# Gate and val of a fused attention and MLP kernel, by 15 products for three token blocks and three weight groups instead of 7 products for two and two

## The chip, the core and the metric

The kernel runs on one core of a Trainium2 chip. The metric is device microseconds of one execution. The engines are named as in the profile: PE multiplies matrices into PSUM (8 banks of 128 x 512 float32), DVE, ACT and POOL do elementwise work, SP issues every DMA of this kernel from one queue, in program order; a DMA is carried out by 16 DMA engines. Each engine runs its own instructions in the order in which they stand, and waits on semaphores for the others.

## What is computed

Blockwise attention (chunks of 64 keys) feeds two MLP layers. The change is in the second, the gated one: gate and val are two products with the same input, of width 1536.

```python
def _moe_ref(x, w_in, w_out):
    h = np.maximum(x @ w_in, 0.0)
    return (h * h @ w_out).astype(np.float32)

def _moe2_ref(x, w_gate, w_val, w_out):
    gate = 1.0 / (1.0 + np.exp(-(x @ w_gate)))
    val = x @ w_val
    return (gate * val @ w_out).astype(np.float32)

# x: 4608 tokens x 512; w_in 512 x 2048, w_out 2048 x 512
# w_gate, w_val 512 x 1536, w_out 1536 x 512
```

All inputs and results are float32, the weights in the layout of 64-bit words from which the kernel makes float32 itself.

## The kernel before

Every float32 product is made of three products of split operands: `split` (L466 to L487) has ACT round a tile to fp32r (L479) and DVE subtract to get the rest (L484), so an operand is twice as large as its float32 tile: 512 KB for 128 x 512. One product of the fast schemes below is six matmuls: two halves of 128 of its 256 inputs, each high x high, rest x high, high x rest (L689 in `multiply`, L1097 in `Long`).

Four stages follow each other on PE: attention together with the first layer's `w_in` (384 columns), the first layer's `w_out` (`Long`, L1097), gate and val (`Unit`, L689), and the last product (`Long` again). All use a scheme with 7 products for a 2 x 2 x 2 block product, in place of 8. For gate and val that is: two groups of 128 features, 512 inputs as two halves, two blocks of 512 tokens. The nine token blocks are four pairs and one single block, which is cut into two halves of 256 columns. There are six such feature groups for each of gate and val (`G2` = 6).

The order of the work is not written out. `Plan` records every instruction as a job with a cost, and `Plan.run` places the jobs on a modelled time axis; what comes out is each engine's instruction order, nothing else of the model reaches the chip. A DMA counts there with its `size` / 270e3 us on one queue, and its due time with `size` / 200e3 us; `look` says how early a load may take its buffer. In `Plan.run` a DVE or POOL job marked `shared` waits for the other engine's.

Weights of gate and val: `prepared` calls `weight_group`, which has two tiles made to float32 (`to_float32`; its last step is one POOL instruction of 512 columns, L551), makes four sums on POOL (L493, tile `ws`), splits them into operands (`wx`), and writes these to DRAM (`ad`, `through_dram`). In `seq`, three feature groups at a time stay in SBUF for all token blocks (`halves`, `order`): each weight operand is read back from DRAM once. The token operands are made per pair by `token_ops`, with subtractions on POOL, and once more for the second half of the groups.

A `Unit` accumulates its 7 products in three PSUM banks; ACT copies out the part sums (L464), DVE adds banks onto them (L493). `units` interleaves two units, so that a bank is rarely used by two products in a row. `finish2` has ACT make the sigmoid and POOL multiply gate and val (L493), and writes the result to DRAM (`ud`).

## Time and profile before

| what | before |
|---|---|
| median of 3 runs | 1601.63 us (1601.32 to 1601.82) |
| the profiled execution | 1601.8 us |
| its span, first to last instruction | 1600.0 us |
| PE / DVE / ACT / POOL busy | 1584.4 / 1306.6 / 972.0 / 530.8 us |
| DMA, mean over the run | 208 GB/s |
| granted TensorE clock | 1.00 throughout |

A stage is read by its window: the busy time of each engine in it, the granted clock, the mean busy share of the 16 DMA engines and the GB/s that they moved. An engine whose busy time is near the window's length has no room there. Whether PE was kept waiting is read from the table of waits. The first layer's `w_out` runs from about 473 to 819 us, gate and val from 818.9 to 1336.9 us.

### The profile page before, as it was taken

What the parts mean: (1) busy time and instruction counts of PE and PEld (TensorE: products, weight loads), DVE (VectorE), ACT (ScalarE), POOL (GpSimd) and SP (SyncE); (2) the same over time, 40 slices, a digit from 0 to 9 for tenths busy, and PEclk for the clock granted to TensorE, in tenths of its full rate; (3) what the DMA queues carried; (4) which work ended last, traced back from release to release, by engine and by line L of the source; (5) the groups of instructions that cost most, each with busy time, mean ns of one, the idle gap of its engine ahead of it and who ended that gap; (6) DMA issues with size and microseconds to landing.
All of it is one profiled execution on the core that took longest, in us unless ns stands there. A gap on an engine that the chain in (4) does not pass through costs nothing.

```text
span 1600.0 us, 29686 instructions
## 1 busy us (share of the span) xinstructions
PE 1584.4 (99%) x10209; PEld 1387.7 (87%) x10209; DVE 1306.6 (82%) x2170; ACT 972.0 (61%) x1922; POOL 530.8 (33%) x432
## 2 busy tenths in 40 slices
PE   8999999999999999999999999999999999999999
PEld 6998999999998888899888898888888888888888
DVE  6968878797989998999998797743786748889886
ACT  7986676676876656566665665543565545555554
POOL 2452402021442111111266685643576641000000
PEclk9999999999999999999999999999999999999999
DMA  9965667677884848487787547586447577866562
GB/s 214 275 166 143 155 190 187 175 207 218 267 290 148 276 152 261 155 280 241 255 279 267 183 146 244 186 281 217 168 162 245 196 260 257 250 196 164 150 174 52
DMA packets 381991, 333.27 MB, mean 208 GB/s; under 512 B 231824, under 2 KB 292240, under 8 KB 381840
## 3 DMA queue, kind: packets, MB, share of 16 engines
q1 hardware_dynamic: 381840, 331.38, 67.8%
q8 instruction: 80, 1.31, 0.4%
q14 instruction: 71, 0.58, 0.1%
HBM read 209.13 MB, written 122.16 MB: 207 GB/s over the span
## 4 chain that ended last, share of the span: by engine, by line
PE 92%; DVE 3%; ACT 2%; DMA 1%; SPq 1%; issue 1%; POOL 0%; DVEq 0%; ACTq 0%
PE bank L689 51%; PE bank L1097 37%; SPq L457 1%; PE bank L878 1%; PE bank L940 1%; PE bank L924 1%; PE bank L858 1%; DMA wraw__750<-in_moe_w_in_dram 0%; DMA wf<-wf__3185 0%; PE bank L1077 0%; DMA k__326<-in_k_dram 0%; DVE T__2019 L484 0%; DMA gd<-b__3834 0%; DVE B__760 L484 0%; DMA ql__4671<-in_q_dram 0%
## 5 line engine op out<-in xcount | busy, mean ns | idle before, releaser
L551 POOL TENSOR_TENSOR wf__6958<-wf__6958,wr__6912 128x512 int32<-128x512 int32 x18 | 28.2, 1568 | 163.1 <-DVE wf__6958 L544 119.8
L551 POOL TENSOR_TENSOR wf__3185<-wf__3185,wr__3118 128x512 int32<-128x512 int32 x16 | 21.8, 1361 | 174.0 <-DVE wf__3185 L544 120.1
L551 POOL TENSOR_TENSOR wf__7071<-wf__7071,wr__6912 128x512 int32<-128x512 int32 x18 | 25.4, 1413 | 99.0 <-DVE wf__7071 L544 73.2
L493 POOL TENSOR_TENSOR raw__523<-raw__724,raw__523 128x384 f32<-128x384 f32 x20 | 24.2, 1229 | 30.1 <-DVE B__653 L484 12.3
L530 ACT ACTIVATE wr__6912<-wr__6912 128x512 int32<-128x512 uint32 x36 | 23.9, 665 | 0.0
L484 DVE TENSOR_TENSOR wx__7016<-ws__7143,wx__7016 128x512 fp32r<-128x512 f32 x18 | 17.8, 988 | 6.0 <-ACT wx__7016 L479 6.0
L493 POOL TENSOR_TENSOR ws__7143<-wf__7071 128x256 f32<-128x256 f32 x12 | 12.5, 1038 | 30.5 <-DVE wx__7684 L484 29.9
L484 DVE TENSOR_TENSOR wx__7684<-ws__7143,wx__7684 128x512 fp32r<-128x512 f32 x18 | 17.9, 997 | 4.7 <-ACT wx__7684 L479 4.7
L484 DVE TENSOR_TENSOR wx__7154<-wf__7071,wx__7154 128x256 fp32r<-128x256 f32 x18 | 14.2, 787 | 3.5 <-ACT wx__7154 L479 3.5
L479 ACT ACTIVATE wx__7154<-wf__7071 128x256 fp32r<-128x256 f32 x18 | 7.4, 411 | 15.8 <-POOL wf__7071 L551 15.6
L493 POOL TENSOR_TENSOR ws__7143<-ws__7143,wf__6958 128x256 f32<-128x256 f32 x18 | 16.2, 898 | 1.2
L533 DVE TENSOR_SCALAR wf__7071<-wf__7071 128x512 f32<-128x512 f32 x18 | 11.8, 653 | 5.6 <-ACT wf__7071 L526 5.4
L533 DVE TENSOR_SCALAR wf__6958<-wf__6958 128x512 f32<-128x512 f32 x18 | 10.3, 572 | 6.3 <-ACT wf__6958 L526 6.3
L493 POOL TENSOR_TENSOR ws__7143<-wf__6958,wf__7071 128x256 f32<-128x256 f32 x18 | 15.3, 848 | 0.3
L526 ACT ACTIVATE wf__3185<-wr__3118 128x512 f32<-128x512 f32 x16 | 10.6, 664 | 6.9 <-DMA wf<-wf__3185 6.9
L904 DVE TENSOR_REDUCE mx__379<-bank 128x4 f32<-128x256 f32 x16 | 6.6, 415 | 10.0 <-PE bank L878 10.0
L526 ACT ACTIVATE wf__7071<-wr__6912 128x512 f32<-128x512 f32 x18 | 11.9, 662 | 4.4 <-DMA wr__6912<-in_moe_w_gate_dram 1.9
L544 DVE SCALAR_TENSOR_TENSOR wf__6958<-wr__6912,wf__6958 128x512 int32<-128x512 int32 x18 | 14.1, 781 | 0.2
L533 DVE TENSOR_SCALAR wf__3185<-wf__3185 128x512 f32<-128x512 f32 x16 | 8.1, 506 | 7.5 <-ACT wf__3185 L526 7.5
L544 DVE SCALAR_TENSOR_TENSOR wf__7071<-wr__6912,wf__7071 128x512 int32<-128x512 int32 x18 | 13.8, 766 | 0.3
L526 ACT ACTIVATE wf__6958<-wr__6912 128x512 f32<-128x512 f32 x18 | 11.9, 659 | 3.1 <-DVE wod__6685 L484 1.5
L904 DVE TENSOR_REDUCE mx__2010<-bank 128x4 f32<-128x256 f32 x16 | 6.7, 417 | 8.5 <-PE bank L878 8.5
(5753 smaller groups left out, 6044.5 us busy)
## 6 DMA issues: line engine op xcount, KB each, us to landing
ad<-wx__7016 SPq DMA_DIRECT2D x27, 512.0 KB, 4.1
ad<-wx__7684 SPq DMA_DIRECT2D x27, 512.0 KB, 5.1
wr__3118<-in_moe_w_out_dram SPq DMA_DIRECT2D x16, 512.0 KB, 4.6
wr__6912<-in_moe_w_gate_dram SPq DMA_DIRECT2D x12, 512.0 KB, 4.7
wr__6912<-in_moe_w_val_dram SPq DMA_DIRECT2D x12, 512.0 KB, 4.4
wr__6912<-in_moe_w_out_dram SPq DMA_DIRECT2D x12, 512.0 KB, 3.9
ad<-wx__7154 SPq DMA_DIRECT2D x18, 256.0 KB, 3.7
wf<-wf__3185 SPq DMA_DIRECT2D x16, 256.0 KB, 4.5
```

Source lines behind the costliest of these rows:

```text
L457: nc.sync.dma_start(out=a, in_=b)
L484: lambda: nc.vector.tensor_tensor(out=lo(), in0=at(src, n, F32, off), in1=hi().bitcast(F32), op=ALU.subtract),
L493: eng, cost(eng, n), lambda: e.tensor_tensor(out=o(), in0=a(), in1=b(), op=op),
L526: nc.scalar.activation(out=at(w), in_=t[:, :, 1].bitcast(F32), func=ACTF.Abs)
L530: nc.scalar.activation(out=low, in_=low.bitcast(U32), func=ACTF.Copy, scale=2.0**-29)
L533: nc.vector.tensor_scalar_max(at(w), at(w), TINY)
L544: nc.vector.scalar_tensor_tensor(out=wi, in0=words()[:, :, 1], scalar=-0x40000000, in1=wi, op0=ALU.bitwise_and, op1=ALU.bitwise_or,)
L551: nc.gpsimd.tensor_tensor(out=wi, in0=wi, in1=words()[:, :, 0], op=ALU.add)
L689: nc.tensor.matmul(out=o, lhsT=at(op, P, F32R, wi * size + half * HB + kk * P), rhs=at(xb, n, F32R, xi * xsize + off), start=(first and kk ...
L858: nc.tensor.transpose(out=at(ps, P, F32, hp * P), in_=at(r, P, F32, hp * P), identity=ident)
L878: nc.tensor.matmul(out=o[c][to, hp, :], lhsT=qv[part, hp, tok], rhs=kv[part, hp, tok], start=True, stop=True,)
L1097: nc.tensor.matmul(out=at(ps[m], n), lhsT=at(w, P, F32R, wi * size + half * HB + m * P), rhs=at(x, n, F32R, xi * n), start=(first and kp = ...
```

## The change

Gate and val are computed in blocks of 3 token blocks x 3 feature groups x 2 halves of the inputs. That takes 15 products in place of 18. Nine token blocks are three such triples (`THREES`), so that none is cut; twelve groups of 128 features are four such groups (`G3` = 4), each for gate and for val. `STEPS` lists the 15 products in their order: product number, PSUM bank, whether the bank is opened, and what is read out afterwards ("c" an ACT copy, "a" a DVE add, "f" a finished tile).

All weight operands are made first, by `weights3`: three tiles to float32 (POOL, as before), sums by `RIGHT_SUMS` on DVE, 256 columns wide, splits, and a write to DRAM (`wd3`) of 256 KB each, for gate and val apart. Nothing of them stays in SBUF: `Group3.run` reads one operand of 512 KB (gate and val side by side) for each of its 15 steps, 180 loads in all. `tokens3` makes the 30 token operands once for each triple, its sums on DVE. The product of gate and val moves from POOL to DVE. In the accounting of `Plan`, the transfers of this stage, and the loads of the stages beside it (`g`, `u`), count at 0.6 of their bytes.

```diff
+STEPS = [
+   (13, 2, True, [('c', 'x1', 2, 1)]),
+   (6, 0, True, [('a', 'x1', 'x1', 1, 0, -1), ('f', 'o6', 's', 'x1', 1, 0)]),
+   (11, 5, True, [('c', 'x2', 5, 1), ('c', 'x3', 5, -1)]),
+   (1, 0, False, [('a', 'x2', 'x2', 1, 0, -1)]),
+   (3, 0, False, [('a', 'x3', 'x3', 1, 0, 1), ('f', 'o4', 's', 'x3', 1, 0)]),
...
-                        [gb[f, b] for b in range(a // BL1, (a + n - 1) // BL1 + 1)], [t], size=P * n * 4, look=13.0)
+                        [gb[f, b] for b in range(a // BL1, (a + n - 1) // BL1 + 1)], [t], size=P * n * 4 * 0.6, look=13.0)
...
+        LAST = [*PAIRS[::-1], (0,)]
+        THREES = [(3, 4, 5), (6, 7, 8), (0, 1, 2)]
+        G3 = F2 // 3
+        raws3, chunks3 = [sbuf(2 * BLK, "wr") for _ in range(2)], [sbuf(BLK, "wf") for _ in range(3)]
+        sums3 = [sbuf(HB, "ws") for _ in range(2)]
+        ops3 = [Buf(8 * HB, name="wx", op=True) for _ in range(5)]
...
+        def weights3(g, m):
+            src = (wg, wv)[m]
+            have = {}
+            for c in range(3):
+                w = to_float32(columns(src, g + c * G3), f"w{m}", (500.0,500.0,500.0,500.0)[g], (raws3, chunks3))
+                for r in range(2):
+                    have[r * 3 + c] = (w, r * HB)
...
+            def get(v):
+                if v not in have:
...
+                    binary("DVE", word(v), a, b, op, HB, [o[0]], reads)
+                return have[v]
+
+            for p, *_ in STEPS:
+                v = RIGHT[p]
+                b, off = get(v)
+                op = ops3[0]
+                ops3.append(ops3.pop(0))
+                if p in TURNED:
+                    turned_split(op, b, off)
+                else:
+                    split(op, b, HB, off=off)
...
+                dma(lambda p=p: wd3[g, p][:, m * BLK:(m + 1) * BLK], lambda op=op: at(op, None, F32), [op], [wb3[g, p]],
+                    size=P * 8 * HB * 0.6, soon=8.0)
...
+        ahead[0] = 260.0
+        for g in range(G3):
+            for m in range(2):
+                weights3(g, m)
...
+        def tokens3(js):
...
+                        dma(lambda t=t: at(t), lambda a=j * BLK, m=2 * r + kk: yd[:, m, a:a + BLK],
+                            y_of(2 * r + kk, j * BLK, BLK), [t], size=P * BLK * 4 * 0.6, look=60.0)
...
+                        binary("DVE", lambda oo=oo: at(oo), lambda aa=aa: at(aa), lambda bb=bb: at(bb), op, BLK, [oo], {oo, aa, bb} if dead else {aa, bb})
...
+        def product3(ps, w, m, xs, first):
+            def go():
+                o = at(ps, BLK)
                 for kk in range(2):
+                    for i, (wi, xi) in enumerate(((0, 0), (1, 0), (0, 1))):
+                        nc.tensor.matmul(
...
+            job("PE", 6 * per, go, [w, *xs] if first else [w, *xs, ps], [ps], stream="main")
...
+            def run(self):
+                for p, c, first, todo in STEPS:
+                    w = Buf(8 * BLK, name="w3", op=True)
+                    dma(lambda w=w: at(w, None, F32), lambda p=p: wd3[self.g, p], [wb3[self.g, p]], [w],
+                        size=P * 8 * BLK * 0.6, look=15.0)
+                    for m in range(2):
+                        if first:
+                            self.banks[m][c] = psum("M")
+                        product3(self.banks[m][c], w, m, self.xs[p], first)
+                        for step in todo:
+                            self.step(m, step)
...
-                    binary("POOL", u.words(gate), u.words(t), u.words(gate), ALU.mult, n, [gate], [gate, t], soon=4.0)
...
+                    binary("DVE", words(gate), words(t), words(gate), ALU.mult, BLK, [gate], [gate, t], soon=4.0)
...
+                dma(lambda: ud[f, j], lambda: at(gate), [gate], [d], size=P * BLK * 4 * 0.6, soon=6.0)
+
+        for js in THREES:
+            xs = tokens3(js)
+            for g in range(G3):
+                Group3(js, g, xs).run()
```

How the order of three engines changes. In the rows, a tile's name is followed by its size in bytes in a partition, its place in SBUF and its buffer number; `x3` are token operands, `w3` weight operands, `wf` the float32 tiles, `wr` the raw ones, `x` and `g` operands and tiles of the first layer's `w_out`.

PE at the start of gate and val, before:

```order
L689 MATMUL bank1_73<-B11_4096_120832__9423,g0_4096_186368__9277 128x512 x3
L689 MATMUL bank1_73<-B11_4096_59392__9435,g0_4096_186368__9277 128x512 x3
L689 MATMUL bank5_77<-B21_4096_75776__9472,g0_4096_186368__9277 128x512 x3
L689 MATMUL bank5_77<-B21_4096_145408__9476,g0_4096_186368__9277 128x512 x3
L689 MATMUL bank7_79<-T1_4096_2048__9458,g0_4096_92160__9280 128x512 x3
L689 MATMUL bank7_79<-T1_4096_83968__9582,g0_4096_92160__9280 128x512 x3
```

and in the change, the fourth and fifth step (products 1 and 3 of `STEPS`, for gate and for val):

```order
L1474 MATMUL bank7_79<-x3_4096_55296__9769,w3_4096_100352__9699 128x512 x3
L1474 MATMUL bank7_79<-x3_4096_63488__9775,w3_4096_100352__9699 128x512 x3
L1474 MATMUL bank4_76<-x3_4096_55296__9769,w3_4096_100352__9699 128x512 x3
L1474 MATMUL bank4_76<-x3_4096_63488__9775,w3_4096_100352__9699 128x512 x3
L1474 MATMUL bank7_79<-x3_4096_22528__9721,w3_4096_47104__9724 128x512 x3
L1474 MATMUL bank7_79<-x3_4096_133120__9726,w3_4096_47104__9724 128x512 x3
```

Two products that accumulate in the same bank, with a DVE add from that bank between them, now stand only one product apart.

SP where the weights of the first groups are brought back, before:

```order
L457 DMA v1_4096_190464__9700<-ad12_235 128x1024
L457 DMA g1_4096_182272__9716<-ad10_233 128x1024
L457 DMA v1_4096_157696__9730<-ad13_236 128x1024
L457 DMA g1_2048_176128__9753<-ad11_234 128x512
L457 DMA v1_4096_153600__9759<-ad14_237 128x1024
L457 DMA ud0_1_98<-e_2048_71680__9683 128x512
L457 DMA v1_2048_110592__9783<-ad15_238 128x512
L457 DMA ad17_240<-wx_4096_34816__7684 128x1024
```

and in the change, near the end of the third weight group of the first triple:

```order
L481 DMA wd3_3_6_269<-wx_2048_178176__6887 128x512
L481 DMA wd3_3_13_268<-wx_2048_176128__6900 128x512
L481 DMA wd3_3_11_270<-wx_2048_180224__6936 128x512
L481 DMA yr_2048_122880__10904<-yd_96 128x512
L481 DMA yr_2048_47104__10906<-yd_96 128x512
L481 DMA yr_2048_49152__10918<-yd_96 128x512
L481 DMA w3_4096_96256__10932<-wd3_3_6_269 128x1024
L481 DMA w3_4096_169984__10196<-wd3_3_13_268 128x1024
L481 DMA wd3_3_1_271<-wx_2048_182272__6972 128x512
L481 DMA w3_4096_10240__9750<-wd3_3_11_270 128x1024
```

An operand of the last weight group is written to DRAM and read back within a few rows of the queue.

POOL in the first layer's `w_out`, before, with the last step of two float32 conversions and the sums of a weight group:

```order
L551 TENSOR_TENSOR wf_2048_102400__6958<-wf_2048_102400__6958,wr_4096_47104__6912 128x512
L551 TENSOR_TENSOR wf_2048_174080__7071<-wf_2048_174080__7071,wr_4096_47104__6912 128x512
L493 TENSOR_TENSOR ws_4096_178176__7143<-wf_2048_174080__7071 128x256
L493 TENSOR_TENSOR ws_4096_178176__7143<-ws_4096_178176__7143,wf_2048_102400__6958 128x256
L493 TENSOR_TENSOR ws_4096_178176__7143<-wf_2048_102400__6958,wf_2048_174080__7071 128x256
```

and DVE in the change, in the same stage:

```order
L508 TENSOR_TENSOR x_4096_161792__6949<-g_2048_110592__6554,x_4096_161792__6949 128x512
L517 TENSOR_TENSOR ws_1024_18944__6897<-wf_2048_174080__6746,wf_2048_45056__6770 128x256
L508 TENSOR_TENSOR wx_2048_180224__6936<-wf_2048_45056__6770,wx_2048_180224__6936 128x256
L508 TENSOR_TENSOR x_4096_47104__6456<-g_2048_192512__6398,x_4096_47104__6456 128x512
L508 TENSOR_TENSOR wx_2048_182272__6972<-ws_1024_51200__6962,wx_2048_182272__6972 128x256
L508 TENSOR_TENSOR wx_2048_184320__7001<-ws_1024_18944__6897,wx_2048_184320__7001 128x256
L517 TENSOR_TENSOR ws_1024_51200__6962<-wf_2048_174080__6746,wf_2048_45056__6770 128x256
L508 TENSOR_TENSOR x_4096_169984__6621<-g_2048_26624__6415,x_4096_169984__6621 128x512
```

The sums of the weights (`ws`) now stand on DVE, between the splits that `w_out`'s products wait for.

## Rows read from the trace of the kernel before

**Rows 1.** The page's first part: span, busy time, share and instructions of each engine.

```profile
span 1600.0 us, 29686 instructions
PE 1584.4 (99%) x10209; PEld 1387.7 (87%) x10209; DVE 1306.6 (82%) x2170; ACT 972.0 (61%) x1922; POOL 530.8 (33%) x432
```

**Rows 2.** Windows: w_out, gate and val's first 164 us, its rest.

```profile
core 0: us, PE busy (x) PEld busy (x) DVE busy (x) ACT busy (x) POOL busy (x), PEclk, DMA share, GB/s
473.00:819.00 346.00, 346.00 (x1687) 293.57 (x1686) 328.63 (x546) 211.05 (x392) 65.98 (x52) 1.00 0.69 226
...
819.00:983.00 164.00, 164.00 (x844) 140.89 (x843) 138.21 (x171) 100.03 (x192) 113.77 (x83) 1.00 0.61 208
983.00:1336.00 353.00, 352.93 (x1673) 297.18 (x1671) 227.51 (x309) 183.05 (x347) 193.70 (x151) 1.00 0.64 222
```

**Rows 3.** PE's waits from 480 us to the end: total, times, longest.

```profile
PE bank L1442 <- ACT d__16418 L464: 0.2, 1, 0.2
```

**Rows 4.** PE in order of time, gate and val: start, duration, engine, line, tiles.

```profile
818.92 0.84 PE L689 MATMUL bank<-B__9423,g__9277 128*128 128x512 f32 x3
819.60 0.84 PE L689 MATMUL bank<-B__9435,g__9277 128*128 128x512 f32 x3
820.28 0.84 PE L689 MATMUL bank<-B__9472,g__9277 128*128 128x512 f32 x3
...
1314.17 0.88 PE L689 MATMUL bank<-B__13490,g__11622 128*128 128x256 f32 x6
1314.89 0.88 PE L689 MATMUL bank<-B__13493,g__11622 128*128 128x256 f32 x6
...
1336.86 1.55 PE L1097 MATMUL bank<-x__6896,o__13403 128*128 128x512 f32 x6
```

**Rows 5.** DVE in order of time, in w_out.

```profile
545.92 0.68 DVE L484 TENSOR_TENSOR x__7084<-g__6461,x__7084 128x512 fp32r<-128x512 f32 x1
546.52 0.68 DVE L493 TENSOR_TENSOR g__6573<-g__6573,g__6381 128x512 f32<-128x512 f32 x1
...
550.32 1.80 DVE L484 TENSOR_TENSOR x__6896<-g__6616,x__6896 128x512 fp32r<-128x512 f32 x1
552.13 1.13 DVE L484 TENSOR_TENSOR x__6669<-g__6251,x__6669 128x512 fp32r<-128x512 f32 x1
...
727.72 0.41 DVE L484 TENSOR_TENSOR x__8220<-g__8396,x__8220 128x256 fp32r<-128x256 f32 x1
728.05 0.41 DVE L484 TENSOR_TENSOR x__8786<-g__8399,x__8786 128x256 fp32r<-128x256 f32 x1
...
729.90 0.42 DVE L537 TENSOR_SCALAR wf__7071<-wf__7071 128x512 int32<-128x512 int32 x1
730.24 0.69 DVE L484 TENSOR_TENSOR x__7687<-g__8609,x__7687 128x512 fp32r<-128x512 f32 x1
```

**Rows 6.** POOL in order of time, beside the DVE rows at 550 us.

```profile
550.02 1.55 POOL L551 TENSOR_TENSOR wf__7071<-wf__7071,wr__6912 128x512 int32<-128x512 int32 x1 [14.81 <-DVE wf__7071 L544]
```

**Rows 7.** Windows of 5 and 10 us in which the DMA engines were busiest.

```profile
1345.00:1350.00 5.00, 5.00 (x23) 4.14 (x23) 4.93 (x9) 3.39 (x6) 0.00 (x0) 1.00 1.03 417
1270.00:1275.00 5.00, 5.00 (x24) 4.14 (x23) 3.51 (x5) 2.54 (x5) 1.71 (x2) 1.00 1.00 393
480.00:485.00 5.00, 5.00 (x23) 4.13 (x22) 3.59 (x6) 2.72 (x6) 0.00 (x0) 1.00 1.04 383
1030.00:1035.00 5.00, 5.00 (x24) 4.14 (x23) 2.43 (x4) 2.28 (x5) 1.29 (x1) 1.00 1.01 356
1340.00:1350.00 10.00, 10.00 (x45) 8.28 (x45) 9.93 (x17) 5.56 (x10) 0.00 (x0) 1.00 0.96 350
680.00:690.00 10.00, 10.00 (x46) 8.29 (x45) 9.84 (x18) 5.61 (x13) 2.50 (x3) 1.00 0.97 322
```

**Rows 8.** DMA issues of the page: size, median us from issue to landing.

```profile
ad<-wx__7016 SPq DMA_DIRECT2D x27, 512.0 KB, 4.1
ad<-wx__7684 SPq DMA_DIRECT2D x27, 512.0 KB, 5.1
wr__6912<-in_moe_w_val_dram SPq DMA_DIRECT2D x12, 512.0 KB, 4.4
...
ad<-wx__7154 SPq DMA_DIRECT2D x18, 256.0 KB, 3.7
```

**Rows 9.** PE, then DVE, in order of time: a product, and the add that reads its bank.

```profile
1081.14 0.84 PE L689 MATMUL bank<-T__11509,v__10243 128*128 128x512 f32 x3
1081.82 0.84 PE L689 MATMUL bank<-T__9804,g__11495 128*128 128x512 f32 x3
...
1082.02 0.69 DVE L493 TENSOR_TENSOR s__11747<-s__11747,bank 128x512 f32<-128x512 f32 x1 [0.67 <-PE bank L689]
```

More of the change, by code (lines that the diff above doesn't have):

```diff
@@ new lines, in tile_attention_relu2_glu, with __init__, used @@
+        taken.extend([*raws3[1:], *chunks3, *sums3, *ops3])
+        steps_of = {id: (x, y, {"+": ALU.add, "-": ALU.subtract}[o]) for id, x, y, o in (*LEFT_SUMS,)}
+        sums_of = {id: (x, y, {"+": ALU.add, "-": ALU.subtract}[o]) for id, x, y, o in (*RIGHT_SUMS,)}
+        class Sums:
+            def __init__(self, of, wanted):
+                self.of, self.left = of, {}
+                for v in wanted:
+                    self.left[v] = self.left.get(v, 0) + 1
+                for x, y, _ in of.values():
+                    self.left[x] = self.left.get(x, 0) + 1
+                    self.left[y] = self.left.get(y, 0) + 1
+            def used(self, v):
+                self.left[v] -= 1
+                return not self.left[v]
@@ new lines, in words, with turned_times, __init__, step @@
+        def words(b):
+            return lambda: at(b, BLK)
+        def turned_times(o, ob, a, b, ib):
+            job("DVE", cost("DVE", BLK), lambda: nc.vector.scalar_tensor_tensor(
+                out=o(), in0=a(), scalar=-1.0, in1=b(), op0=ALU.mult, op1=ALU.mult), ib, ob,
+                shared=not any(x.psum for x in ib))
+        class Group3:
+            def __init__(self, js, g, xs):
+                self.js, self.g, self.xs = js, g, xs
+                self.banks, self.bufs, self.gates = [{}, {}], [{}, {}], {}
+            def run(self):
[9 more added lines that the diff above has]
+                            self.step(m, step)
+            def step(self, m, step):
+                kind, bufs, banks = step[0], self.bufs[m], self.banks[m]
+                if kind == "c":
+                    _, d, c, sign = step
+                    bufs[d], ps = sbuf(BLK, "c"), banks[c]
+                    copy(words(bufs[d]), [bufs[d]], words(ps), [ps], BLK, scale=float(sign))
+                elif kind in "az":
+                    _, d, a, sa, b, sb = step
+                    x, y = bufs[a], bufs[b] if kind == "z" else banks[b]
+                    if d not in bufs:
+                        bufs[d] = sbuf(BLK, "c")
+                    if sa != sb and sa < 0:
+                        x, y = y, x
+                    binary("DVE", words(bufs[d]), words(x), words(y), ALU.add if sa == sb else ALU.subtract, BLK,
+                           [bufs[d]], [x, y])
+                else:
+                    self.finish(m, *step[1:])
+            def finish(self, m, name, kind, what, sign, *left):
+                i, c = divmod(int(name[1:]), 3)
+                t = self.bufs[m][what] if kind == "s" else self.banks[m][what]
@@ L1355, in finish @@
                 if m == 0:
-                    src = t if t is not None else u.U
-                    t = t if t is not None else sbuf(n, "s")
-                    copy(u.words(t), [t], u.words(src), [src], n, func=ACTF.Sigmoid, soon=3.0)
-                    gates[row, col] = t
+                    gate = sbuf(BLK, "s") if kind == "b" or left[0] else t
+                    copy(words(gate), [gate], words(t), [t], BLK, func=ACTF.Sigmoid, soon=3.0, scale=float(sign))
+                    self.gates[name] = gate
@@ L1367, in finish @@
+                f, j = self.g + c * G3, self.js[i]
                 d = Buf(name="u")
                 ub.setdefault((f, j), []).append(d)
[L1369 to L1383 removed]
```

146 lines of the change are left out of this document (86 added, 60 removed), and 10 rows, old and new, of the table STEPS.

## The prediction

> **What bounds the kernel now.** I read the page's first part first: PE is busy for 99% of the span, and the next engine, DVE, for 82% [rows 1]. Shares are averages, so the windows of the stages come next: in `w_out`, in the first 164 us of gate and val and in their rest, PE is busy for the whole window at a granted clock of 1.00, which is the 2.4 GHz level [rows 2]. The table of waits confirms it: from 480 us to the end PE waits once, for 0.2 us [rows 3]. So PE alone sets the time of this stage, matmuls taken away are gained in full, and every other cost counts only so far as it makes PE wait. Three things have little room: DVE in `w_out`, busy for 329 of 346 us [rows 2]; POOL beside it, which slows it (below); and the DMA engines, at a share of 0.6 to 0.7 [rows 2].
>
> **The matmuls (certain).** In the instruction lists, gate and val before are 2016 matmuls of 512 columns and 504 of 256; after, 3 triples x 4 groups x 2 sides x 15 products x 6 = 2160 of 512 columns. All other matmuls are the same in number and size. A row of three 512-column matmuls starts 0.68 us after the one before it, one of six 256-column matmuls 0.72 us [rows 4]: 0.2267 and 0.12 us each. Before: 2016 x 0.2267 + 504 x 0.12 = 517.5 us, and the trace has 1336.86 - 818.92 = 517.9 [rows 4]. After: 2160 x 0.2267 = 489.7. That is **-27.8 us** if PE never waits.
>
> **The weight stream.** Before, an operand is read once and stays; after, 180 loads of 512 KB cross the queue, one for each pair of products, so 0.5 MB per 2.72 us, beside writes of operands, results, token loads and raw weights. The whole stage moves about 176 MB in 490 us, 360 GB/s, against 208 and 222 before [rows 2]. It is not even. On SP, between the load for a step of the first triple (issued after 26 products of the stage) and the load of the second triple that product 128 needs, stand 60 transfers of 512 KB and 99 of 256 KB (58 operand writes, 29 result writes, 12 token loads): 57.4 MB for 102 products of 1.36 us = 138.7 us, so 414 GB/s is wanted. At less, the last load of the stretch is late by 57.4 MB / rate - 138.7 us, and PE stands for that long in all, since SP issues in order and PE multiplies in order.
>
> What the DMA engines can hold is not shown over such a length; the nearest rows are the windows in which they were full. Five-microsecond windows at a share of 1.00 to 1.04 moved 417, 393, 383 and 356 GB/s, ten-microsecond windows at 0.96 and 0.97 moved 350 and 322 [rows 7]. At 417 nothing is late (-1); at 350, which is 365 at full share, 18 to 25 us; at the worst window's 332 at full share, 34. I take the short windows' range as the nearest in kind (mostly 4 KB rows, reads with some writes), and 380 in it, near the 387 that is their mean and a little lower because the stretch holds 87 writes: 57.4 MB / 380 GB/s = 151.1, **+12 us**, bounds 0 and 34. That factor of 0.6 in the ordering's accounts costs nothing by itself; it lets the order ask for 414 where the full bytes would have spread the loads.
>
> The Trainium skill ("DMA: Bandwidth & Descriptors", Specifications) gives one core about 358 GB/s of HBM, below a fabric ceiling of 435; by that figure the stretch would take an estimated 160 us, 22 us late, and the sum would come out at an estimated 1603. The 417 window [rows 7] is above that figure, so it is no hard limit here. Another page of the Trainium skill, "HBM Reference" (Specifications), says that a core streaming alone reaches about 425; by it the term would be 0 and the sum an estimated 1581.
>
> **DVE.** Weight sums go from POOL to DVE, in 256 columns; token sums and the product of gate and val too. A DVE instruction starts 0.60 us after the one before for 512 columns (545.92 to 546.52), 0.33 for 256, and 0.34 for the one-tile word operations [rows 5]. At these pitches `w_out`'s 543 instructions (412 of 0.60, 107 of 0.335, 24 of 0.34) are 292 us; it was busy for 328.6, so 36.6 us more, with POOL busy for 66.0 [rows 2]: 0.55 us for each microsecond of POOL. One place shows it: beside a POOL row of 1.55 us from 550.02 [rows 6] a DVE row lasts 1.80 instead of 0.68 [rows 5]. After, the same stretch has 648 instructions (408 of 0.60, 211 of 0.335, 29 of 0.34), 326 us, but only 18 POOL instructions in place of 52, 21 us x 0.55 = 11: 337 of 345 us. The first triple has 316 instructions in place of 166, 156 us, and 14 us of POOL x 0.55 = 8: 164 of 163. Later there is room (394 instructions, 227 of 326 us). So DVE is just full for 500 us, and by these sums 1 us short in the triple.
>
> A full engine also answers late. At products 1 and 3 of `STEPS` (24 places) a bank is used again one product later, with an add from it between: the add starts 0.88 us after the product's last row starts and lasts 0.69 [rows 9], ending 1.57 after it; the next product on the bank starts 0.68 + 1.36 = 2.04 after that row. The 0.47 us left are gone if DVE is in another instruction of 0.60 or stretched by POOL. If half of 24 places lose 0.2 us, that is 2.4. With the triple's 1 us I take **+3**, bounds 0 and 16; the 16 is the case that DVE can't give up the idle 17 us that it has in `w_out` [rows 2], because it waits for loads and ACT there.
>
> **Write and read back.** In the first triple the last weight group is written just before it is read: the second half of one operand is released after product 83 and wanted by product 90, another after 90 and wanted at 98, 7 or 8 products, 9.5 to 10.9 us. The chain is a split on DVE of 0.33 us that queues behind some others (1.2), a write of 256 KB that lands in 3.7 and a read of 512 KB, for which the 512 KB rows have 4.1 to 5.1 [rows 8]: 9 to 10 us at a DMA share of 0.61 [rows 2], so at a full share it is short. SP waits in order at the write, and the loads behind it go late with it. I take **+4**, bounds 0 and 10, partly the same microseconds as the stream's.
>
> **What goes the other way for nothing.** POOL loses the sums, but PE never waits for POOL [rows 3], so no gain beyond the DVE account. ACT gets 44 small copies in `w_out` on a busy time of 211 of 346 [rows 2]: hidden. Less raw work late in the stage hides under PE too.
>
> **Sum.** The profiled execution took 1601.8 us, 0.2 above the median: 1601.8 - 27.8 + 12 + 3 + 4 = **1593.0**.
>
> **Rivals.**
> 1. *Clean*: the DMA engines hold 400 to 417 GB/s over the whole stretch and the rest is hidden. For it: the 417 window was full without any loss [rows 7]. Against: the other full windows. 1601.8 - 27.8 + 0 to 5 + 0 to 1 = 1574 to 1580, centre 1577.
> 2. *The transfers become the bound* (the slower side): the stretch holds only the rate of the lower windows [rows 7]. With 4 + 3 us for the other terms, the time is that of before where the stream is 20.8 us late, which is a rate of 360 GB/s; below 353 it is slower by more than 3.2 us, above 368 faster by as much. At 356 it is 1603.5, at 343 (near the middle of 356 and 332) 1610. For it: writes and reads are mixed as in the 10-us windows. Against: those windows weren't asked for more all the time.
> 3. *DVE becomes the bound*: its idle time in `w_out` and the slow rows beside POOL stay, so it falls 16 us behind instead of 3: 1606. It decides from about 12 us up. For it: 337 of 345 and 164 of 163 us. Against: with fewer POOL rows the long rows of 1.80 [rows 5] become rarer.
>
> That the change doesn't do what it says I give nothing: the counts of matmuls are fixed in the lists.
>
> **How the numbers follow.** Chances: forecast (1585 to 1599) 0.41; clean 0.18; transfers 0.23; DVE 0.13; other combinations 0.05. About 0.2% (3.2 us) is what a measurement of this kernel can tell from no change. Faster than 1598.4: the clean case and nearly all of the forecast, 0.58. Slower than 1604.8: most of transfers (those under 353 GB/s), of DVE and of the rest, 0.28. Between: 0.14. The range from 1578 to 1614 leaves out half of the clean case and the worst ends of rivals 2 and 3, some 0.2.
>
> **What would show it.** PE's busy time in gate and val should be 490 us in 2160 matmuls at line L1474. If the stream costs what I say, PE's waits name the weight tiles `w3` with a DMA as releaser, some 12 us, between about 835 and 990 us, where the windows show a share near 1.0 and 370 to 400 GB/s; without such a wait the clean case holds. If DVE is the bound, its windows from 473 to 990 us are above 0.97 and PE waits for operands `x3` or, at products 1 and 3, for banks read at L517. The write-back shows as SP waiting for `wx` tiles at the `wd3` writes near product 83. I am wrong if PE waits in `w_out` already, if the stall stands in the second or third triple, where the order asks for less, or if the granted clock falls below 1.00 behind the stalls.

## The result: 1.3% slower, and the profile after

The changed kernel takes 1623.18 us (median of 4 runs, 1615.1 to 1626.0) against 1601.58 before: 1.0127 of it, with a 95% interval of 1.0088 to 1.0165. Nothing was gained; 21.6 us were lost. A second set of runs of the same kernel gave 1620.56 us (1619.9 to 1622.3), so below a gain counts from about 1621, and one of 2 or 3 us says nothing. The profiled execution took 1625.4 us.

The page's first part, which answers to [rows 1]:

```profile
span 1623.6 us, 29392 instructions
PE 1575.7 (97%) x9849; PEld 1356.2 (84%) x9849; DVE 1374.8 (85%) x2516; ACT 958.8 (59%) x1920; POOL 242.5 (15%) x214
```

PE now has gaps. The windows of `w_out` and of the three triples (from the first matmul of each) say where; they answer to [rows 2] (busy time of each engine, granted clock, DMA share, GB/s):

```profile
core 0: us, PE busy (x) PEld busy (x) DVE busy (x) ACT busy (x) POOL busy (x), PEclk, DMA share, GB/s
475.00:839.40 364.40, 353.47 (x1681) 291.50 (x1680) 343.48 (x646) 216.34 (x434) 38.83 (x22) 1.00 0.69 235
839.44:1026.00 186.56, 169.90 (x721) 137.21 (x720) 166.19 (x314) 101.61 (x200) 14.42 (x11) 0.97 0.92 344
1026.00:1195.20 169.20, 164.60 (x721) 134.78 (x721) 139.45 (x225) 89.78 (x164) 28.80 (x29) 1.00 0.90 341
1195.20:1360.41 165.21, 164.24 (x721) 134.92 (x721) 111.68 (x178) 72.28 (x127) 6.21 (x6) 1.00 0.89 320
```

By the first and last matmuls of each stage, attention took 473.5 us (472.5 before), `w_out` 364.5 (345.1), gate and val 521.0 (517.9, and 489.7 by the count of matmuls), the last product 259.6 (259.7). So two losses eat the 27.8 us: 19.4 in `w_out`, where PE does the same matmuls as before, and 31.3 in gate and val. +1.0 + 19.4 + 31.3 - 27.8 - 0.1 = 23.8, and the spans differ by 23.6. A triple's 720 matmuls would take 163.2 us without a wait, so of the loss in gate and val 23.4 us stand in the first triple, 6.0 in the second and 2.0 in the third.

These are times of one execution. The same kernel profiled again (e18) had 360.9 us in `w_out` and 522.2 in gate and val, and e2, e3, e4 and e10, which leave `w_out` as it is, had 359.9 to 362.6 there. So the loss in `w_out` is 15 to 19 us, and a difference of some 4 us in one stage's time says nothing alone.

PE's waits from 480 us on, the largest in total, where before there was one of 0.2 us [rows 3] (total, times, longest):

```profile
PE bank L1474 <- DMA w__10196<-wd: 6.0, 1, 6.0
PE bank L1474 <- DVE c__9958 L517: 4.4, 3, 2.1
PE bank L1125 <- DVE x__6949 L508: 3.9, 2, 2.1
PE bank L1125 <- DVE x__7923 L508: 3.6, 4, 2.4
PE bank L1474 <- DVE c__9883 L517: 2.7, 1, 2.7
```

L1125 is `w_out`, L1474 gate and val. All but one name DVE: operands `x` in `w_out`, and in gate and val the adds onto part sums `c`, which empty a bank. The one DMA is a load of weights (`w3`, printed here as `w`).

**In `w_out`** the stretch before one such wait, DVE first, then PE:

```profile
658.85 0.69 DVE L517 TENSOR_TENSOR g__6264<-g__6415,g__6264 128x512 f32<-128x512 f32 x1 [0.44 <-DMA g__6415<-gd]
...
673.64 0.68 DVE L517 TENSOR_TENSOR g__6264<-g__8097,g__6264 128x512 f32<-128x512 f32 x1
674.24 0.68 DVE L508 TENSOR_TENSOR x__7923<-g__7435,x__7923 128x512 fp32r<-128x512 f32 x1
...
671.96 0.61 PE L1125 MATMUL bank<-x__7923,wos__6225 128*128 128x512 f32 x2
674.98 1.19 PE L1125 MATMUL bank<-x__7923,wos__6225 128*128 128x512 f32 x4 [2.41 <-DVE x__7923 L508]
```

From 658.85 us on DVE goes without a gap at one instruction per 0.60 us and is still late with `x__7923`; PE starts as soon as that split is done. Yet DVE stood idle for 364.4 - 343.5 = 20.9 us of this stage, some of it behind loads of `g`, as at 658.85.

**At products 1 and 3** of `STEPS`, PE, then DVE:

```profile
849.64 0.84 PE L1474 MATMUL bank<-x__9775,w__9699 128*128 128x512 f32 x3
853.23 0.50 PE L1474 MATMUL bank<-x__9721,w__9724 128*128 128x512 f32 x1 [2.75 <-DVE c__9883 L517]
...
849.49 0.69 DVE L508 TENSOR_TENSOR x__9864<-ys__9820,x__9864 128x512 fp32r<-128x512 f32 x1
850.09 0.69 DVE L517 TENSOR_TENSOR yr__9461<-yr__9461,yr__9491 128x512 f32<-128x512 f32 x1
850.69 0.68 DVE L517 TENSOR_TENSOR yr__9470<-yr__9470,yr__9501 128x512 f32<-128x512 f32 x1
851.29 0.69 DVE L517 TENSOR_TENSOR ys__9684<-ys__9684,yr__9454 128x512 f32<-128x512 f32 x1
851.89 0.68 DVE L517 TENSOR_TENSOR ys__9820<-ys__9820,yr__9456 128x512 f32<-128x512 f32 x1
852.50 0.68 DVE L517 TENSOR_TENSOR c__9883<-c__9883,bank 128x512 f32<-128x512 f32 x1
```

The product on the bank ended at 849.1 us. The add that empties the bank stands behind five instructions, a split and four sums of token operands, and starts at 852.50; in [rows 9] such an add started 0.88 us after the product's last row did.

**At the end of the first triple** the weight load that PE waits for, as the window of 900 to 980 us, the load's issue on SP, and PE around it:

```profile
900.00:980.00 80.00, 70.66 (x305) 56.50 (x303) 73.08 (x148) 45.68 (x96) 10.50 (x8) 1.00 1.02 380
...
976.87 0.38 SPq L481 DMA_DIRECT2D w__10196<-wd  x1
...
975.86 0.84 PE L1474 MATMUL bank<-x__10115,w__9750 128*128 128x512 f32 x3
982.70 1.65 PE L1474 MATMUL bank<-x__9625,w__10196 128*128 128x512 f32 x3 [6.00 <-DMA w__10196<-wd]
984.15 1.48 PE L1474 MATMUL bank<-x__9630,w__10196 128*128 128x512 f32 x3
985.43 1.48 PE L1474 MATMUL bank<-x__9625,w__10196 128*128 128x512 f32 x3
986.71 1.30 PE L1474 MATMUL bank<-x__9630,w__10196 128*128 128x512 f32 x3
987.84 0.85 PE L1474 MATMUL bank<-x__9696,w__10932 128*128 128x512 f32 x3
```

The DMA engines are full for 80 us (380 GB/s at a share of 1.02). The load is issued when PE already needs it. Behind the wait rows of three matmuls stand 1.28 us apart, not 0.68, for 5 us: the granted clock from 980.83 to 987.66 us is 0.50, its lower level, 1.2 GHz, after PE stood for 6 us.

### The profile page after: what moved, and what is told of

Read it like the earlier page. It is cut to its first block, busy times and chain, and to the rows that moved or that the text cites. A ratio compares the mean times of both kernels' runs of the same rounds, so it can differ in the third digit from the quotient of the medians.

```text
span 1623.6 us, 29392 instructions
## 1 busy us (share of the span) xinstructions
PE 1575.7 (97%) x9849; PEld 1356.2 (84%) x9849; DVE 1374.8 (85%) x2516; ACT 958.8 (59%) x1920; POOL 242.5 (15%) x214
## 3 DMA queue, kind: packets, MB, share of 16 engines
q8 instruction: 78, 1.28, 0.3%
## 4 chain that ended last, share of the span: by engine, by line
PE 67%; DVE 15%; DMA 8%; issue 3%; ACT 3%; SPq 1%; POOL 1%; DVEq 0%; ACTq 0%; POOLq 0%
PE bank L1125 29%; PE bank L1474 19%; PE bank L717 17%; SPq L481 1%; DMA ud<-c__9958 1%; DMA wd<-wx__6972 1%; PE bank L968 1%; DMA wd<-wx__7001 1%; PE bank L906 1%; PE bank L952 1%; DMA wf<-wf__3197 1%; PE bank L886 1%; DMA wr__6707<-in_moe_w_gate_dram 1%; DMA w__11065<-wd 1%; DMA wr__6707<-in_moe_w_out_dram 0%
## 5 line engine op out<-in xcount | busy, mean ns | idle before, releaser
L579 POOL TENSOR_TENSOR wf__6746<-wf__6746,wr__6707 128x512 int32<-128x512 int32 x10 | 14.1, 1412 | 270.9 <-DVE wf__6746 L572 127.5
L579 POOL TENSOR_TENSOR wf__3197<-wf__3197,wr__3130 128x512 int32<-128x512 int32 x16 | 21.2, 1325 | 180.0 <-DVE wf__3197 L572 127.7
L517 DVE TENSOR_TENSOR c__11131<-c__11131,bank 128x512 f32<-128x512 f32 x29 | 19.9, 685 | 14.8 <-PE bank L1474 8.3
L579 POOL TENSOR_TENSOR wf__6921<-wf__6921,wr__5457 128x512 int32<-128x512 int32 x10 | 15.5, 1546 | 64.2 <-DMA w__9750<-wd 22.0
L517 DVE TENSOR_TENSOR c__9958<-c__9958,bank 128x512 f32<-128x512 f32 x23 | 15.7, 684 | 10.3 <-PE bank L1474 4.2
L503 ACT ACTIVATE wx__6972<-ws__6962 128x256 fp32r<-128x256 f32 x24 | 10.0, 416 | 19.6 <-DVE ws__6962 L517 9.5
L579 POOL TENSOR_TENSOR wf__6770<-wf__6770,wr__6707 128x512 int32<-128x512 int32 x4 | 6.7, 1687 | 96.5 <-ACT x__8356 L503 38.8
L579 POOL TENSOR_TENSOR wf__6770<-wf__6770,wr__5457 128x512 int32<-128x512 int32 x4 | 7.0, 1756 | 89.1 <-ACT x__7185 L503 55.2
L579 POOL TENSOR_TENSOR wf__6746<-wf__6746,wr__5457 128x512 int32<-128x512 int32 x4 | 9.8, 2443 | 65.9 <-DVE wf__6746 L572 53.2
L579 POOL TENSOR_TENSOR wf__6921<-wf__6921,wr__6707 128x512 int32<-128x512 int32 x4 | 5.8, 1448 | 77.2 <-ACT c__9412 L488 66.6
L488 ACT ACTIVATE c__9958<-c__9958 128x512 f32<-128x512 f32 x13 | 8.2, 631 | 14.6 <-DVE c__9958 L517 14.6
L488 ACT ACTIVATE c__9958<-bank 128x512 f32<-128x512 f32 x15 | 8.9, 593 | 10.8 <-PE bank L1474 9.2
L561 DVE TENSOR_SCALAR wf__3197<-wf__3197 128x512 f32<-128x512 f32 x16 | 7.6, 476 | 9.0 <-ACT wf__3197 L554 9.0
L554 ACT ACTIVATE wf__3197<-wr__3130 128x512 f32<-128x512 f32 x16 | 10.6, 662 | 7.7 <-DMA wf<-wf__3197 7.7
L517 DVE TENSOR_TENSOR c__11507<-c__11507,bank 128x512 f32<-128x512 f32 x12 | 8.2, 687 | 7.2 <-ACT c__12443 L488 3.2
L503 ACT ACTIVATE wx__6900<-ws__6897 128x256 fp32r<-128x256 f32 x24 | 9.9, 412 | 7.6 <-DVE ws__6897 L517 5.9
L986 ACT ACTIVATE raw__535<-bank 128x256 f32<-128x256 f32 x36 | 12.1, 382 | 2.4 <-PE bank L968 2.1
L986 ACT ACTIVATE raw__736<-bank 128x256 f32<-128x256 f32 x36 | 11.7, 392 | 2.7 <-PE bank L968 2.5
```

The source lines that it names most:

```text
L488: lambda: nc.scalar.activation(out=o(), in_=i(), func=func, **kw), ib, ob, soon=soon,
L503: lambda: nc.scalar.activation(out=hi(), in_=at(src, n, F32, off), func=ACTF.Copy),
L517: eng, cost(eng, n), lambda: e.tensor_tensor(out=o(), in0=a(), in1=b(), op=op),
L579: nc.gpsimd.tensor_tensor(out=wi, in0=wi, in1=words()[:, :, 0], op=ALU.add)
L986: nc.scalar.activation(out=o[:, :, a:a + CH], in_=i, func=ACTF.Copy)
```

## Experiments

Theory D: DVE has too little room. Theory T: the transfers. Theory B: the bank used again one product later. Theory W (e10): the write and read back of the last weight group. Most runs keep the order of all engines and shorten instructions or transfers, so that only a duration changes; stage times are those of the profiled execution.

**e1_sums8.** `n` is 8 columns but for the first use of each buffer.

```
- binary("DVE", word(v), a, b, op, HB, [o[0]], reads)
+ ... nc.vector.tensor_tensor(out=w()[:, :n], in0=a()[:, :n], in1=b()[:, :n], op=op) ...
```

> The changed kernel in the same order, but 94 of the 96 weight sums on DVE are made on 8 columns instead of 256 (the operands made from them hold wrong numbers). That takes about 0.26 us x 47 = 12 us from DVE in w_out and as much from the first triple; transfers, POOL, ACT and PE are as in the changed kernel. Theory D (DVE has too little room in w_out and the first triple): w_out falls from 364 to 350-354 us and the first triple by 5 to 10 us, total 1600 to 1607. Theory T (the transfers set the loss): 1618 to 1626, as the changed kernel's 1623.

Measured: 1614.8 us (1613.5 to 1616.4); `w_out` 358.7, gate and val 518.6. About 6 us of the 1621 came back, where D wanted 14 to 21; `w_out` is 2 to 6 us shorter.

**e8_prep8.** The same for the splits and the word steps of these weights.

> The changed kernel in the same order, but all DVE work on the gate and val weights (sums, splits and word steps, about 290 instructions) is made on 8 columns, once each buffer has been written in full; the operands are wrong. It takes about 43 us from DVE in w_out and 35 us from the first triple; ACT, POOL, SP and the bytes stay. Theory D (DVE full in these two stages is the main cause): w_out falls from 364 to 346-350 us, and in the first triple only the wait for a weight tile (6 to 9 us) is left: total 1588 to 1598. Theory T (transfers, coming to PE through DVE's queue): w_out 358 or more, total over 1605.

Measured: 1606.2 us; `w_out` 349.1, gate and val 518.7. The two stages:

```profile
473.60:822.70 349.10, 346.98 (x1682) 292.00 (x1681) 307.31 (x644) 215.93 (x433) 30.26 (x22) 1.00 0.73 245
822.70:1341.00 518.30, 497.82 (x2160) 406.57 (x2159) 382.53 (x718) 263.39 (x493) 49.45 (x46) 0.99 0.92 338
```

With 36 us less of DVE work PE's gaps in `w_out` are gone (347.0 of 349.1). For `w_out` D holds. For gate and val it fails in this form: there DVE has 34 us less to do (417 to 383), the stage is 2 us shorter, which is within the spread, and the loss stays, with 186.8 us in the first triple.

**e2_stream4.**

```
- dma(lambda w=w: at(w, None, F32), lambda p=p: wd3[self.g, p], ...
+ dma(lambda w=w: at(w, HB, F32), lambda p=p: wd3[self.g, p][:, :HB], ...
- lhsT=at(w, P, F32R, m * BLK + wi * HB + kk * P),
+ lhsT=at(w, P, F32R, kk * P),
```

> The changed kernel in the same order, but each of the 180 weight loads brings a quarter of its bytes (1 KB of the 4 KB of a row), and all matmuls of a product use this quarter, so the products are wrong. DVE, ACT and POOL do the same work. Theory T (rate of the DMA engines): nearly all of the 31 us that gate and val lose come back, 1592 to 1598. Theory D (DVE): only the one wait of 6.2 us on a weight tile and the slow clock after it (2.4 us) can come back, 1612 to 1620; w_out stays at 364 us.

Measured: 1610.2 us (1608.3 to 1613.7); gate and val 508.2, `w_out` 362.3. The wait on the weight tile fell to 3.0 us, and most waits that name DVE's adds became shorter too, though nothing of DVE's work was cut: those for `c__9958` from 4.4 to 0.9 us in total, while the one at 851 us stayed (3.1). The first triple is 9.2 us shorter and the second 3.5. So 11 to 13 us are the stream's, more than the one wait that names a DMA: most of the rest had come to PE through DVE's queue. T holds for this part and not for the whole.

**e3_adds13 and e4_adds58.**

```
- self.step(m, step)
+ self.n = 8 if p in (1, 3) and step is todo[0] else BLK; self.step(m, step)
```

> The changed kernel in the same order, but the DVE adds after products 1 and 3 (48 of them, from the bank that is used again one product later) are made on 8 columns instead of 512, so five results of each block are wrong. It takes 0.5 us x 48 = 24 us from DVE, 8 us of them in the first triple, and shortens the wait for the bank. Theory B (the bank's second use one product later): the waits of PE for tiles c at L517, 17 us with the clock after them, go, w_out is unchanged: 1602 to 1608. Theory D alone (only the sum of DVE's work counts): 5 to 8 us come back in the first triple, 1614 to 1619. Theory T: 1618 to 1626.

> Control for the run before: the same number of DVE adds (48) on 8 columns, but those after products 8 and 5, whose bank has two products between its uses or none after. The same 24 us of DVE work go. Theory B: the waits at products 1 and 3 are shorter only where the queue before them was long: 1610 to 1618, at least 5 us more than the run on products 1 and 3. Theory D alone: the same as that run within 3 us.

Measured: e3 1615.7 us (1613.2 to 1619.5), gate and val 514.6; e4 1621.2 us (1618.0 to 1629.0), gate and val 519.2. The same cut of DVE's work gave 6.4 us in gate and val at products 1 and 3, and 1.8, within the spread, elsewhere; the medians are 5.5 us apart. So the place counts (B), but at less than half of the 17 us that I had put on it: a shorter add doesn't come earlier in the queue, and the wait at 851 us stayed at 2.8 us.

**e7_swap.**

```
- for p, c, first, todo in STEPS:
+ for p, c, first, todo in (*STEPS[:4], STEPS[5], STEPS[4], *STEPS[6:]):
```

> The changed kernel with product 7 taken between products 1 and 3 in each group, so that the bank of products 1 and 3 is used again two products later; all results are computed. Theory B (the early second use costs what the run with short adds gave back, 6 to 7 us): the waits for tiles c at L517 fall from 17 to about 8 us, w_out is unchanged, 1614 to 1619. If the waits are only DVE's lateness, they move to other products: 1620 to 1626.

Measured: 1615.1 us (1614.8 to 1617.3), gate and val 514.2, `w_out` 364.4. One more product between the two uses gives the same 6 to 7 us with all results computed. By triples it is clearer: the second and the third took 163.2 us each, which is the count, and the first 187.8. So the early second use is the whole loss of 8 us in the later triples, and in the first, where other causes stand beside it, moving it gave nothing.

**e10_chain.**

```
- lambda p=p: wd3[self.g, p], [wb3[self.g, p]], [w],
+ lambda p=p: wd3[self.g - (self.g == 3 and self.js[0] == 3), p], [wb3[self.g, p]], [w],
```

> The changed kernel in the same order, but in the first triple the last weight group's loads bring the operands of the group before it, which were written long ago, so they don't wait for a write (the results of that group are wrong). Theory W (write and read back): the wait of 6.2 us on a weight tile at 983 us goes, with the slow clock behind it: 6 to 9 us, 1613 to 1618. Against it (the load is late because the queue or DVE before it is late): less than 3 us, and the wait stands at the same product or a few products later.

Measured: 1619.2 us (1615.6 to 1621.0), no gain that the spread lets one see, and the wait stands at the same product:

```profile
PE bank L1474 <- DMA w__10196<-wd: 6.2, 1, 6.2
```

The load no longer needs the late write and is as late as before: SP issued it 1.0 us before PE was ready for it, not 0.2 after, and it took 7.1 us to land, not 5.8. So it isn't the read back; theory W falls. By the issue and landing times of the changed kernel, 5 to 8 transfers (the new one counted) were under way at each issue between 905 and 980 us, mostly 8, where the kernel before mostly had 2 or 3 in that stretch; SP waits for an earlier transfer before nearly every issue.

**e9_all.** The cuts of e8, e2 and e3 together.

> The same order with three cuts at once: the weights' DVE work on 8 columns, a quarter of the bytes of each weight load, and the adds after products 1 and 3 on 8 columns. If DVE's room, the transfers and the bank used again one product later are the whole loss, the kernel comes to 1601.8 - 27.8 = 1574 plus some microseconds: 1574 to 1582. If something else sets a part (ACT, SP's order, the write and read back of the last weight group), 1585 or more, and w_out or gate and val keep waits that name it.

Measured: 1587.2 us (1585.1 to 1590.8), 0.991 of before (0.9895 to 0.9925); `w_out` 349.3, gate and val 500.1. The single gains from 1621, 15 + 11 + 5 = 31, add up to this run's 34. It stays some 13 us above 1574: 4 in `w_out`, 10 in gate and val, of which 3 are rows at half the clock and two waits are these:

```profile
PE bank L1474 <- DMA w__10196<-wd: 3.3, 1, 3.3
PE bank L1474 <- DVE c__9883 L517: 2.4, 1, 2.4
```

**e6_full_bytes and e12_seven_tenths.** All six factors 1.0, or 0.7.

> The changed kernel with all six factors of 0.6 taken out, so the ordering counts the full bytes at its 270 GB/s; same work, another order on all engines. If 0.6 is what makes the order ask for more than the DMA engines hold, the waits at 935 to 985 us go: 1600 to 1612. If the full bytes make the ordering believe that PE waits for transfers, it puts other work in the wrong places relative to the products, and the time rises: 1630 to 1700.

> The changed kernel with all six factors at 0.7 instead of 0.6, so that the ordering believes in 386 GB/s instead of 450; the DMA engines moved 389 to 398 GB/s at a full share in the changed kernel. If the ordering only has to ask for what they hold, the waits between 930 and 985 us become shorter by 5 us or more: 1610 to 1618. If spreading the loads puts other work in the wrong places, as the full bytes did: 1626 to 1650.

Measured: 1791.2 us with full bytes (1790.0 to 1791.3), far beyond the range; nearly all of it is one wait in `w_out`:

```profile
PE bank L1125 <- ACT x__7433 L503: 171.6, 1, 171.6
```

The ordering placed the weights' preparation in front of an operand (of ACT's 162 instructions from 540 to 705 us 112 write `wx`), as expected if it believes that PE will wait for transfers; while PE stands, DVE works on. The windows around it, the first inside the wait:

```profile
560.00:600.00 40.00, 0.00 (x0) 0.00 (x0) 32.54 (x67) 17.05 (x39) 8.15 (x6) 0.50 0.76 262
600.00:760.00 160.00, 63.91 (x268) 51.55 (x269) 130.58 (x250) 79.74 (x162) 19.06 (x13) 0.69 0.71 236
```

`w_out` takes 525.8 us, and then gate and val 493.5, only 3.8 above the count, with the same 180 loads. So the loads alone cost nothing that counts: what costs is that they meet, in the first triple, the raw weights, the operand writes and DVE's work on them. Which of these it is, this run doesn't part. At 0.7: 1620.8 us (1618.3 to 1621.9), no change; the wait on a weight tile grew to 11.0 us and others shrank. A mild change of the factor doesn't bring the time back, and taking it out is far worse.

**e11_loads_full.** Only the factor of the loads of `g` is 1.0.

> The changed kernel, but the token loads g of w_out count their full bytes in the ordering; the other five factors stay at 0.6. If DVE's idle time in w_out (21 us, 12 of them behind loads of g) comes from loads that the ordering places too late, w_out falls by 5 to 10 us: 1612 to 1619. If DVE's sum of work alone sets w_out, it stays within 3 us of 364: 1619 to 1626.

Measured: 1616.1 us (1615.2 to 1619.5): `w_out` 349.5, gate and val 527.1. In `w_out`:

```profile
474.50:824.00 349.50, 347.64 (x1683) 293.45 (x1681) 335.38 (x631) 215.52 (x424) 35.70 (x21) 1.00 0.73 240
```

The loss in `w_out` is gone with most of DVE's work still there: no wait behind a load of `g` over 0.2 us is left, against 2.4, 2.0 and 1.2 as the longest in the changed kernel. But 15 of DVE's instructions also moved from `w_out` into gate and val, which lost 6 us. Of the 15 us in `w_out`, 8 are DVE's work that moved out (343.5 to 335.4 busy) and 7 its idle time (20.9 to 14.1). So the sum of work decides only together with the idle time. Beside each other, from the windows of `w_out`:

| kernel | DVE instructions | DVE busy, us | `w_out`, us |
|---|---|---|---|
| before | 544 | 327.5 | 344.9 |
| changed | 646 | 343.5 | 364.4 |
| e8_prep8 | 644 | 307.3 | 349.1 |
| e11_loads_full | 631 | 335.4 | 349.5 |
| e16_kept_group | 660 | 348.0 | 362.4 |

In every one of these but e8 the stage is DVE's busy time plus 14 to 21 us. That busy and idle time add up to the stage is no finding; that the idle time stays at 14 to 21 us while the work differs by 20 is.

**e13_mult_pool.**

```
- binary("DVE", words(gate), words(t), words(gate), ALU.mult, ...
+ binary("POOL", words(gate), words(t), words(gate), ALU.mult, ...
```

> The changed kernel with the product of gate and val back on POOL (108 of them): DVE has 65 us less of its own, POOL about 150 us more, which by 0.55 us for each microsecond of POOL takes 80 us of DVE's time. If the two share DVE's time in this way, nothing is gained: 1620 to 1632. If DVE's own instructions are what counts, the waits of gate and val shrink by 10 us or more: 1605 to 1615.

Measured: 1631.5 us (1628.1 to 1633.8), 10 us worse; gate and val 529.6, with the longest waits on DVE's adds at 4.7 and 4.6 us. POOL is no relief for DVE: 108 instructions of 0.60 us, 65 us, left DVE, but in gate and val its busy time fell by 10 only (417.4 to 407.1), while POOL's rose from 49.4 to 186.5, so DVE's other instructions took 0.40 us longer for each microsecond of POOL. The Trainium skill ("SBUF — State Buffer", Terms) gives a reason: the two share a port pair that one instruction holds alone, and the other blocks. That agrees with the 1.80 us row beside POOL in [rows 5, 6].

**e14_loads_full_cut.** e11 with the cuts of e2 and e3.

> The order of the run in which the token loads g count their full bytes, with two cuts: a quarter of the bytes of each weight load, and the adds after products 1 and 3 on 8 columns (results wrong). If gate and val lose their time to the weight stream and to the early second use of the bank, it falls from 527 to 500-508 us while w_out stays at 349.5: total 1588 to 1597. If another cause came with this order, gate and val stays above 515: over 1603.

Measured: 1602.7 us (1601.9 to 1605.7); `w_out` 347.7, gate and val 515.1, not 500 to 508. In this order the two cuts take only 12 us out of gate and val. What holds the other 25 was not tried apart: its trace has waits of 4.1 us on a weight tile and of 11 us on DVE's adds, and 6 us of rows at half the clock. DVE's moved work is the likely cause, and that is argued only.

**e15_swap_loads_full, e16_kept_group and e17_kept_group_late.** e15 joins e7 and e11. In e16 the last group's operands go for both sides into one `w3` tile, which the first triple uses in place:

```
+ straight[g, p] = w
+ dma(lambda p=p: wd3[g, p], lambda w=w: at(w, None, F32), [w], [wb3[g, p]], size=P * 16 * HB * 0.6, soon=30.0)
...
- w = Buf(8 * BLK, name="w3", op=True)
+ w = straight.pop((self.g, p), None)
+ if w is None:
...
```

> Token loads g at full bytes and product 7 between products 1 and 3, all results computed. If the two gains add (15 us in w_out less 6 in gate and val; 7 us): 1606 to 1612. If the ordering gives one of them back: 1613 to 1620.

> As the run before, but the operands of the last weight group are made for gate and val side by side and used by the first triple where they are made, in SBUF; they are still written to DRAM for the other triples. 15 loads of 512 KB, 7.9 MB or 20 us at 390 GB/s, and the read back leave the crowded stretch; all results are computed. If the crowd of transfers there is the cause, the wait of 6 to 8 us on a weight tile goes and those around it shrink: 8 to 16 us less than the run before, 1593 to 1602. If the cause is DVE's queue or the order, within 5 us of it or more.

> As the run before, with the raw weights of the last product loaded and prepared up to 180 us later, out of the end of the first triple and the start of the second. If these transfers and their DVE work matter: 2 to 6 us less than the run before. If not: the same within 3 us.

Measured: e15 1609.5 us (1608.1 to 1610.3), the two gains add; `w_out` 348.0, gate and val 522.2. e16 1598.7 us (1596.9 to 1601.2, 10 runs), 0.9979 of the kernel before (0.9970 to 0.9988): the only version with all results computed that beats both, by 0.2% and by 1.4%. e17, with the last product's raw weights later, 1600.4 us (1597.4 to 1603.0), the same within the spread. The stages of e16:

```profile
473.30:835.70 362.40, 352.60 (x1681) 290.51 (x1681) 347.96 (x660) 221.48 (x443) 43.84 (x23) 1.00 0.74 244
835.70:1333.00 497.30, 493.18 (x2161) 404.30 (x2161) 408.10 (x703) 258.76 (x482) 48.56 (x45) 1.00 0.91 332
```

Gate and val is down by 25 us to 497.3, 7.6 above the count; no wait names a weight load, and the clock is 1.00 throughout. The third weight group of the first triple, 59.4 us in e15 and 54.5 in the changed kernel, takes 40.8, the count. With the read back excluded by e10 (in the changed kernel's order), what is left is the 15 loads fewer in the crowded stretch and the DVE work that moved ahead of it; the run doesn't part the two. `w_out` has 35 DVE instructions more than in e15 (660 to 625) and is longer by 14 us: its loss is back.

**e18_changed_again.**

> The changed kernel again, nothing edited. If its first four runs were typical, the median is 1620 to 1625 with runs from 1615 to 1627, and the waits in w_out (19 us over 345), at products 1 and 3 and at the weight tile near 980 us stand at the same places. A median under 1617 would make the gains of 2 to 8 us in the other runs uncertain.

Measured: 1620.6 us, 1.0118 of before (1.0101 to 1.0135); `w_out` 360.9, gate and val 522.2, waits at the same places (the one on the weight tile is 8.0 us). The gains of e1, e3 and e7 (5 to 6 us) stand; that of e10 does not.

## Why the prediction was wrong, by its steps

I forecast 1593, a gain of 8.8, with a range up to 1614. It was slower by 21.6.

- **The matmuls, -27.8: right.** Rows still stand 0.68 us apart where PE doesn't wait, and with the causes cut, gate and val comes to 497 to 500 us.
- **The weight stream, +12: right in size and rate, and in place for the most part.** e2 gives 11 to 13, of which 9 are in the first triple, and e6 that it takes the loads and the writes of the first triple together, as in the stretch that I counted; the wait names a weight tile at 983 us, inside the 835 to 990 that I gave; the engines held 380 GB/s over 80 us, which is the figure I took. The form was not as I drew it: I expected PE to wait for `w3` for 12 us, and 6 did; most of the rest arrived as late adds of DVE. That the size came out with that form is in part luck. The Trainium skill's 358 GB/s for one core ("DMA: Bandwidth & Descriptors", Specifications) was passed again, over a longer stretch.
- **Write and read back, +4: wrong as a cause.** e10 takes the write away, and nothing moves that the spread lets one see. The time is the stream's, counted twice.
- **DVE, +3: this is the step that failed.** I set 337 us of work against 345 and took the 17 us in which DVE had been idle [rows 2] as free to fill, against the sentence that bounded the term by 16. DVE filled none: it was busy for 343.5 and idle for 20.9, and 343.5 + 20.9 = 364.4 is the stage (342.8 + 18.1 in e18). So `w_out`, which I put at nothing, lost 15 to 19 us. My own numbers, with the idle time kept, gave 337 + 17 - 345 = +9 in `w_out` alone. The busy time was short as well: I counted 18 POOL instructions of 21 us, and there were 22 of 38.8. The mechanism was my rival 3, at 0.13, and its 16 us were short too; its sign, DVE's windows above 0.97, would have missed it, for they are at 0.94 in `w_out` and 0.89 in the first triple. The idle time is of DVE's queue: each engine takes its rows in order, and in the kernel before, too, DVE stood with work behind the row that waited.
- **Products 1 and 3: the mechanism was right, the size too small.** I priced a delay of one instruction, 0.2 us at 12 places. At 849 us five instructions stood ahead of the add. By e3 and e7 it is 6 to 7 us, not 2.4. Part of it stands in the second and third triple, which I had named as a sign of being wrong: 8 us were lost there, and e7 gives them back.
- **The sign I gave for being wrong, PE waiting in `w_out` already, is what the trace shows.** The 0.6 I costed at nothing "by itself"; e11 shows that the part of it on the loads of `g` makes them late. Without it `w_out` is 15 us shorter, 7 by less idle time and 8 by work that moved into gate and val, where 6 are lost again.
- **The clock: named as a sign, priced at nothing.** Rows at half rate behind the longer waits cost 1.6 us in `w_out` and 4.0 in gate and val.

By single cuts, in gate and val: 13 us of the 31 are the stream, 6 the early second use of the bank, 2, within the spread, the weights' work on DVE; the last 10 (e9) are the slow clock and waits that no run isolates. Where the weights are ready beforehand (e6) nearly all of it is gone, but at a far higher price elsewhere. Why e14's order keeps 25 us stays open.

## What to carry to other kernels

An engine that follows a fixed order can keep its idle time when it gets more work, as DVE did here (17 us before, 18 to 21 after): set busy time plus today's idle time against the stage, not busy time alone. A wait that names one engine can have been handed on by another, so cut transfers and work apart before believing the name. And look what stands in the queue ahead of an instruction that frees a bank, not only how long that instruction takes.

## What the runs showed of the hardware beyond that

- With the DMA engines full, landing times grew: a write of 256 KB took 6.4 us between 900 and 985 us against 3.7 before [rows 8], a weight load of 512 KB 6.9 in the median of 22 (4.8 to 9.7) against 4.1 to 5.1 for transfers of that size in [rows 8].

```profile
wd<-wx__6887 SPq DMA_DIRECT2D x9, 256.0 KB, 6.4
w__9750<-wd SPq DMA_DIRECT2D x4, 512.0 KB, 6.5
...
w__10127<-wd SPq DMA_DIRECT2D x2, 512.0 KB, 9.0
```

- A wait of PE of 1.8 us, to 754.69 us in `w_out`, was followed by rows at the lower clock level (0.43 us between single matmuls, not 0.23) for some 3 us, while after waits of 2.1 and 2.4 us, at 593 and 675 us, the rows went on at 0.23. The window of the first:

```profile
740.00:760.00 20.00, 18.16 (x116) 16.39 (x116) 18.14 (x40) 10.44 (x26) 2.60 (x2) 0.91 0.89 290
```
